# An early one-element gelu, two sums of halves behind a later product, and second-layer fills in four column tiles

## The chip, the cores and the metric

The kernel runs on one core of a Trainium2 chip. The core's engines work side by side, each from its own queue: PE (TensorE: matmuls, with its weight loads shown as PEld), DVE (VectorE), ACT (ScalarE), POOL (GpSimd) and SP (which here only issues DMAs). The metric is the device time of one execution in microseconds (us), the median of several runs. Before the change it is 344.38 us, the median of three runs (344.12 to 345.33).

## The reference

The kernel computes causal attention with a forgetting factor, and a two-layer perceptron with a tanh-gelu on its output.

```
q, k, v: (8, 8, 576, 64)   f: (8, 8, 576)   w_in: (512, 2048)   w_out: (2048, 512)
scores = q k^T / sqrt(64) + cum[query] - cum[key],  cum = cumsum(log(clip(f)))   (causal)
attn   = exp(scores - max) / (sum + 1e-09)
x      = (attn v), heads beside each other            -> (4608, 512)
h      = x @ w_in
g      = 0.5 h (1 + tanh(sqrt(2/pi) (h + 0.044715 h^3)))
out    = g @ w_out                                     -> (4608, 512) float32
```

Inputs and output are float32; the kernel multiplies in bfloat16 and accumulates in float32.

## The kernel before

**Attention** goes by quads, four heads of one batch at a time: 16 quads in all. For a quad `i`, `scores(i, r)` (line 224) makes the transposed scores in three rounds r = 0, 1, 2 of 512 columns each. Its matmuls have 32 rows, one head to each of the four row strips of the array. ACT then takes the exponential of each round with two instructions (line 232), into the tile `pt`. Masks on the diagonal run on POOL (line 238) or DVE. `denominators(i)`, called D, and `attn_out(i, x)`, called V and run for x = 0 and 1, multiply `pt` with the decay column or with the weighted values (line 292). Their matmuls have 128 rows and 32 (or 1) columns, one head to each of the four column strips: 24 matmuls each. Both write the PSUM tile `po`, of which there is one. DVE empties it: two transposes and a reciprocal behind D (lines 311 to 315), a product behind V (line 323), which writes `xT`, the input of the perceptron.

**The first layer** goes by chunks of 512 tokens: nine chunks, c = 0 to 8. `mlp_in(c, prs)` (line 334) makes 256 of the 2048 hidden features per call, with eight matmuls of 128x128 by 512, and ACT applies the gelu (line 341) into `gT`. Its PSUM tiles `ps_h` share two buffers (pool `psS`) with the scores.

**The second layer** of chunks 1 to 8 is one level of Strassen's scheme in Winograd's form: seven products of halves instead of eight. DVE prepares sums of halves: `weight_sums` once for the weights, and `gelu_sums(half, which)` for each chunk, in two halves of the features, each with four instructions. They are numbered 1 (`g1`, line 376), 2 (`g2`, line 378), 3 (the difference that takes the place of `a21` in `gT` and is read as `d1`, line 380) and 4 (`g4`, line 382), and run in the order 1, 3, 2, 4. `seven_products(c)` is a generator. Each step of it, called a fill here, is one matmul of 128x128 by 256 (line 397). A product takes 16 fills and a chunk 112. The products come in a fixed order: 1 is `a11 w11`, 2 is `a12 w21`, 3 is `g2 u2`, 4 is `d1 w3`, 5 is `g1 u1`, 6 is `a22 u4` and 7 is `g4 w22`. Two PSUM tiles `pa` and `pb` take turns. When a product ends, DVE copies it (`keep`, line 413), adds a kept copy to it or writes it out (`result`, lines 418 and 420), and SP starts the store. So product 3, which goes on in `pa`, has to wait until the copy of product 1 (`keep("p1", pa)`) is made.

**The order** is written out by hand, and each engine follows it in its own queue. For the first chunks it stands in the table FRONT: `S` is scores, `D` and `V` as above, `I` and `J` the first layer, `G` gelu_sums, `U` weight_sums, `F.c.n` and `f.c.n` n fills of chunk c, `X` load_exp. After FRONT a loop runs over c = 2 to 8. It makes the fills left over of chunk c-1, the eight `mlp_in` calls with `prepare` and the loads in between, the sums, and then the attention of two quads (`pair`), with the fills of chunk c between its parts. In `pair(i, j, c)` the order is S(i,0) D(j) 22 fills, S(i,1) V(j,0) 18, S(i,2) V(j,1) 16, S(i+1,0) D(i) 18, S(i+1,1) V(i,0) 9 V(i,1) 7, S(i+1,2). Ten fills stand ahead of it and the last 12 follow it. For c = 6 there is no quad i+1, and the second part is D(i) 18 V(i,0) V(i,1) 18. Chunks 7 and 8 have no attention beside them.

**Tables of ACT.** Exponentials and gelus need different function tables, and a change of table is an instruction of its own (ACT_TABLE_LOAD), put ahead of the first instruction that needs it. `load_exp` (line 196) is an exponential of one element, put ahead of the first real one, so that the table comes early. There is nothing of the kind for gelu.

**Column tiles.** A fill can be made in a second form. When the list `by_columns` is not empty, each fill becomes four matmuls of 128 rows and 32 columns, each with its own weight load, on the four column strips of the array. `out_part(c, n, tiled)` sets the list, and the table's word `f` calls it with tiled = 1. Before the change only some fills of chunk 0 (512 wide, line 459) are made so.

Of the kernel before, what the change touches and what calls it, by code (L numbers as in the profile page):

```python
# [10 lines left out]
AF = mybir.ActivationFunctionType  # L11
# [5 lines left out]
def kernel(  # L17
# [10 lines left out]
    nc = tc.nc  # L28

    B, H, S, D = q.shape  # L30
# [47 lines left out]
        LX.1.0@WO.2 TK.2 J.0.2 J.1.2 X LK.4 F.0.6 TK.3 B.3.256 S.2.0 LK.5 F.0.9 S.2.2 F.0.10 S.2.1 TQ.3 TQ.4 F.0.10 LV.2.0@LK.5 m.2.1 vw.2  # L78
        TK.4 S.3.0 f.0.1 M.2.2 CL.2 LQ.5 M.2.0 D.2 f.0.6 S.3.1 m.3.0 F.0.6 V.2.0 S.3.2 TK.5 LK.6 M.3.2 f.0.7 V.2.1 CL.3
        S.4.1 m.3.1 LQ.6 F.0.6 TQ.5 H.4.2.1 D.3 H.4.0.1 LQ.7 VW.4 H.4.0.0 V.3.1 v.3.0 f.0.3 H.4.2.0 CL.4 I.1.0 m.4.1 U.0 LV.2.1@LQ.5 I.1.4  # L80
        TQ.6 m.4.2.3 I.1.1 I.1.5 U.1 LV.3.0@LQ.7 m.4.2.2 TK.6 G.0 M.4.0 I.1.2 I.1.3 U.3 I.1.6 I.1.7 G.1 U.2 X F.1.14 S.5.0 F.1.28 S.5.1 D.4 M.5.0 F.1.16
        S.5.2 V.4.0 m.5.2.3 F.1.10 VW.5 V.4.1 CL.5 m.5.2.2 LQ.8 S.6.0 F.1.10 M.5.1 D.5 F.1.7 S.6.1 V.5.1 F.1.12 V.5.0 vw.6 S.6.2
        m.6.1 M.6.2.2 m.6.0 m.6.2.3 LK.7 LK.8 CL.6 LX.3.1@LK.6
    """

# [8 lines left out]
    def many(n, shape, dtype, name):  # L94
        return [singles.tile(shape, dtype, name=f"{name}{i}") for i in range(n)]
# [11 lines left out]
    vw = many(2, [128, NT + 1, 4, D], BF16, "vw")  # L107
# [13 lines left out]
    shift = singles.tile([128, 1], FP32, name="shift")  # L121
    idle = singles.tile([128, 512], BF16, name="idle")
    spare = singles.tile([1, 1], FP32, name="spare")
# [70 lines left out]
    def load_exp():  # L194

        nc.scalar.activation(spare, shift[0:1, :], AF.Exp)

    idle_ps = []

# [168 lines left out]
    def gelu_sums(half, which=(1, 3, 2, 4)):  # L368

        n = HF // 2  # L370
        f0, f1 = slice(n * half, n * half + n), slice(HF + n * half, HF + n * half + n)
        a11, a12 = gT[:, f0, 0:HC], gT[:, f1, 0:HC]
        a21, a22 = gT[:, f0, HC:CH], gT[:, f1, HC:CH]
        for k in which:
            if k == 1:
                nc.vector.tensor_add(g1[:, f0], a21, a22)  # L376
            if k == 2:
                nc.vector.tensor_sub(g2[:, f0], g1[:, f0], a11)
            if k == 3:
                nc.vector.tensor_sub(a21, a11, a21)  # L380
            if k == 4:
                nc.vector.tensor_sub(g4[:, f0], a12, g2[:, f0])

    def seven_products(c):

        r0, last = CH * c, c == NCH - 1
        a11, a12 = gT[:, 0:HF, 0:HC], gT[:, HF:, 0:HC]
        d1, a22 = gT[:, 0:HF, HC:], gT[:, HF:, HC:]
        w11, w3 = w_out_sb[:, 0:HF, 0:HD], w_out_sb[:, 0:HF, HD:]
        w21, w22 = w_out_sb[:, HF:, 0:HD], w_out_sb[:, HF:, HD:]  # L390

        def multiply(ps, x, w, first, then, ns=range(2), cols=(0, HD)):
            for n in ns:
                for j in range(HF):
                    width = 32 if by_columns else 128
                    for c0 in range(0, 128, width):
                        nc.tensor.matmul(ps[c0:c0 + width, n, cols[0]:cols[1]],  # L397
                                         x[:, j, 128 * n + c0:128 * n + c0 + width],
                                         w[:, j, cols[0]:cols[1]],
                                         start=(first and n == ns[0] and j == 0), stop=(j == HF - 1),  # L400
                                         skip_group_check=True)
                    if n == ns[-1] and j == HF - 1:
                        then()
                    yield

        def bank():
            return psM.tile([128, 2, HD], FP32, name="ps_w", tag="m")

        kept = {}

        def keep(name, ps):
            kept[name] = snap_pool.tile([128, 2, HD], FP32, name="snap", tag="snap")
            nc.vector.tensor_copy(kept[name], ps)  # L413

        def result(i, j, x, y=None):
            st = ostage_pool.tile([128, 2, HD], FP32, name="o_st", tag="o")
            if y is None:
                nc.vector.tensor_copy(st, x)
            else:
                nc.vector.tensor_add(st, x, y)  # L420
            nc.sync.dma_start(
                out=out[r0 + HC * i:r0 + HC * (i + 1), HD * j:HD * (j + 1)].rearrange("(n p) d -> p n d", p=128),
                in_=st)

        def corner():
            keep("v4", pa)
            result(1, 1, kept["p7"], kept["v4"])

        def piece(ps, n, cols):
            st = ostage_pool.tile([128, 2, HD], FP32, name="o_st", tag="o")  # L430
            s = slice(*cols)
            nc.vector.tensor_add(st[:, n, s], ps[:, n, s], kept["v4"][:, n, s])  # L432
            eng = nc.scalar if cols[0] else nc.sync
            eng.dma_start(out=out[r0 + 128 * n:r0 + 128 * n + 128, HD + cols[0]:HD + cols[1]], in_=st[:, n, s])

        pa, pb = bank(), bank()
        yield from multiply(pa, a11, w11, True, lambda: keep("p1", pa))
        yield from multiply(pb, a12, w21, True, lambda: result(0, 0, pb, kept["p1"]))
        yield from multiply(pa, g2, u2, False, lambda: keep("v2", pa))
        yield from multiply(pb, d1, w3, True, lambda: keep("p7", pb))  # L440
        yield from multiply(pa, g1, u1, False, corner)
        yield from multiply(pb, a22, u4, False, lambda: result(1, 0, pb, kept["v2"]))
        if not last:
            yield from multiply(pa, g4, w22, False, lambda: result(0, 1, pa))
            return
        for n, cols in ((0, (0, HD)), (1, (0, HD // 2)), (1, (HD // 2, HD))):
            ps = bank()
            yield from multiply(ps, g4, w22, True, lambda: piece(ps, n, cols), (n,), cols)

    def mlp_out(c):  # L450

        for n in range(CH // 128):
            r0 = CH * c + 128 * n
            st = ostage_pool.tile([128, D_MODEL], FP32, name="o_st", tag="o")
            pso = psM.tile([128, D_MODEL], FP32, name="pso", tag="m")
            for ft in range(N_FT):
                cols = 32 if by_columns else 128
                for c0 in range(0, 128, cols):
                    nc.tensor.matmul(pso[c0:c0 + cols, :],
                                     gT[:, ft, 128 * n + c0:128 * n + c0 + cols],  # L460
                                     w_out_sb[:, ft, :],
                                     start=(ft == 0), stop=(ft == N_FT - 1), skip_group_check=True)
                if ft == N_FT - 1:
                    nc.vector.tensor_copy(st, pso)
                    nc.sync.dma_start(out=out[r0:r0 + 128, :], in_=st)
                yield
# [61 lines left out]
    def pull(it, n):  # L528
        for _ in range(n):
            if next(it, False) is False:  # L530
                return
# [4 lines left out]
    def out_part(c, n, tiled=0):  # L536
        by_columns[:] = [True] * tiled
        pull(fills.setdefault(c, seven_products(c) if c else mlp_out(c)), n)
# [5 lines left out]
    def load_values(b, half):  # L544
# [31 lines left out]
        "I": lambda c, pr: mlp_in(c, (pr,)),  # L576
        "J": mlp_in_half,
        "U": weight_sums,
        "G": gelu_sums,
        "F": out_part,  # L580
        "f": lambda c, n: out_part(c, n, 1),
        "B": keep_busy,
        "X": load_exp,
    }

    def run(table):
# [10 lines left out]
    def beside(i, r, c, todo):  # L597

        if i is not None:
            scores(i, r)  # L600
        for n, x in enumerate(todo):
            if isinstance(x, int):
                out_part(c, x)
            else:
                x()
            if n == 0 and i is not None:
                after_scores(i, r)

    def after_scores(i, r):
        mask(i, r)  # L610
        if r == 1:
            make_vw(i, nc.gpsimd)
        if r == 2:
            copy_low(i)
# [25 lines left out]
    with tc.manual_schedule():  # L640
        setup()
        run(FRONT)
        for c in range(2, NCH):
            out_part(c - 1, CH)
            for pr in (0, 1):
                mlp_in(c, (pr,))
            if c + 1 < B:
                prepare(2 * c + 3, 2 * c + 4)
            if c + 2 < B:
                load_v(c + 2)  # L650
            for pr in (4, 5):
                mlp_in(c, (pr,))
            gelu_sums(0)
            for pr in (2, 3, 6, 7):
                mlp_in(c, (pr,))
            gelu_sums(1)
            if c + 1 < B:
                load_exp()
                out_part(c, 10)
                pair(2 * c + 3, 2 * c + 2, c)  # L660
        out_part(NCH - 1, CH)
# [30 lines left out]
```

## Time and profile before

The profiled execution took 344.71 us, of which its span, from the first to the last instruction, is 343.0 us. It lies 0.33 us over the median of the runs, so a difference worked out against the profiled execution is taken off the median as it is.

| engine | busy us | share of the span | instructions |
|---|---|---|---|
| PE | 322.6 | 94% | 3748 |
| PEld | 196.5 | 57% | 3768 |
| DVE | 199.3 | 58% | 307 |
| ACT | 191.2 | 56% | 201 |
| POOL | 110.6 | 32% | 155 |

The granted clock of PE is 0.996 of full speed on the mean. In the profile's lines the first number is the start and the second the time that the group took, both in us, then come engine, line, operation, output and inputs, tile (rows*columns for PE), shape and count. In square brackets stands how long the engine sat idle ahead of the group and what ended that. Matmuls are pipelined and their ends are modelled: the row of a matmul of 512 columns lasts 0.379 us, while the next one starts 0.2156 us behind it. So the pace is read from starts. A gap in the pipeline is a little longer than the idle time shown.

### The profile page before, as it was taken

What the parts mean: (1) busy time and instruction counts of PE and PEld (TensorE: products, weight loads), DVE (VectorE), ACT (ScalarE), POOL (GpSimd) and SP (SyncE); (2) the same over time, 40 slices, a digit from 0 to 9 for tenths busy, and PEclk for the clock granted to TensorE, in tenths of its full rate; (3) what the DMA queues carried; (4) which work ended last, traced back from release to release, by engine and by line L of the source; (5) the groups of instructions that cost most, each with busy time, mean ns of one, the idle gap of its engine ahead of it and who ended that gap; (6) DMA issues with size and microseconds to landing.
All of it is one profiled execution on the core that took longest, in us unless ns stands there. A gap on an engine that the chain in (4) does not pass through costs nothing. (4 is left out here: it accounts for less than half of the span.)

```text
span 343.0 us, 8601 instructions
## 1 busy us (share of the span) xinstructions
PE 322.6 (94%) x3748; PEld 196.5 (57%) x3768; DVE 199.3 (58%) x307; ACT 191.2 (56%) x201; POOL 110.6 (32%) x155
## 2 busy tenths in 40 slices
PE   3999999999899999999999999999999999989984
PEld 1458844445564466546654676456745774575574
DVE  4785059876686686737664566556634760452363
ACT  4784676777446566657466664675566605503500
POOL 8997470600506234601651145106410410000000
PEclk9999999999999999999999999999999999999998
DMA  7999999560316960490039211910110111002002
GB/s 131 218 221 179 204 226 212 98 154 2 65 44 127 226 145 31 117 216 10 32 112 201 58 33 65 212 26 32 51 45 0 34 36 59 1 32 92 0 32 92
DMA packets 44310, 33.21 MB, mean 97 GB/s; under 512 B 27488, under 2 KB 37856, under 8 KB 44272
## 3 DMA queue, kind: packets, MB, share of 16 engines
q0 software_dynamic: 8848, 16.58, 26.9%
q1 hardware_dynamic: 35280, 16.01, 17.4%
q8 instruction: 29, 0.48, 0.6%
q14 instruction: 9, 0.07, 0.1%
q10 hardware_dynamic: 144, 0.07, 0.1%
HBM read 36.85 MB, written 9.44 MB: 135 GB/s over the span
## 5 line engine op out<-in xcount | busy, mean ns | idle before, releaser
L232 ACT ACTIVATE pt<-ps_s 128x1024 bf16<-128x1024 f32 (+2 forms) x100 | 93.7, 988 | 52.9 <-PE ps_s L224 40.8
L334 PE MATMUL ps_h<-xT,w_in_sb 128*128 128x512 bf16 x496 | 111.8, 379 | 5.1 <-ACT gT L341 4.3
L341 ACT ACTIVATE gT<-ps_h 128x1024 bf16<-128x1024 f32 x64 | 64.9, 1024 | 51.4 <-PE ps_h L334 45.5
L334 PEld LDWEIGHTS <-w_in_sb 128*128 128x128 bf16 x512 | 49.9, 98 | 64.3 <-issue 6.4
L238 POOL TENSOR_SCALAR_AFFINE_SELECT pt<-pt 128x512 bf16<-128x512 bf16 (+3 forms) x65 | 38.4, 601 | 143.2 <-ACT pt L232 142.3
L397 PEld LDWEIGHTS <-gT 128*128 128x128 bf16 x512 | 48.3, 98 | 9.5 <-issue 0.2
L376 DVE TENSOR_TENSOR gsum<-gT 128x1024 bf16<-128x1024 bf16 x16 | 11.1, 692 | 66.3 <-ACT gT L341 66.3
L397 PE MATMUL ps_w<-w_out_sb,gT 128*128 128x256 bf16 x384 | 46.6, 273 | 0.0
L397 PEld LDWEIGHTS <-gsum 128*128 128x128 bf16 x392 | 36.3, 98 | 10.8 <-issue 5.4
L224 PE MATMUL ps_s<-qT,kT 32*128 32x64 bf16 (+5 forms) x896 | 36.9, 264 | 0.3 <-ACT pt L232 0.2
L397 PE MATMUL ps_w<-usum,gsum 128*128 128x256 bf16 x256 | 32.0, 273 | 3.5 <-DVE snap L413 3.5
L182 POOL TENSOR_TENSOR vw<-v_nat,wT 128x1280 bf16<-128x1280 f32 (+1 forms) x13 | 30.0, 2310 | 0.1
L165 DVE STREAM_TRANSPOSE kT<-k_c 128x576 f32<-128x576 f32 x16 | 19.9, 1247 | 16.0 <-DMA k_c<-in_k_dram 15.8
L413 DVE COPY snap<-ps_w 128x512 f32<-128x512 f32 x32 | 21.6, 676 | 12.9 <-PE ps_w L397 12.9
L224 PEld LDWEIGHTS <-kT 32*128 32x128 bf16 x896 | 17.0, 93 | 17.3 <-issue 11.5
L323 DVE TENSOR_TENSOR xT<-po,rb 128x576 bf16<-128x576 f32 x26 | 19.6, 754 | 11.9 <-PE po L292 11.8
L292 PE MATMUL po<-pt,vw 128*32 128x64 bf16 (+4 forms) x624 | 22.5, 279 | 0.3 <-DVE xT L323 0.3
L165 DVE STREAM_TRANSPOSE qT<-q_c 128x576 f32<-128x576 f32 x16 | 19.9, 1244 | 1.8 <-DMA q_c<-in_q_dram 1.1
L292 PEld LDWEIGHTS <-vw 128*32 128x32 bf16 x672 | 13.6, 96 | 12.2 <-issue 5.5
L341 ACT ACT_TABLE_LOAD x7 | 9.0, 1283 | 16.3 <-issue 16.3
L397 PE MATMUL ps_w<-usum,gT 128*128 128x256 bf16 x128 | 17.0, 273 | 0.0
L136 POOL DMA_DIRECT2D v_nat<-in_v_dram x20 | 15.3, 778 | 5.0 <-DMA w_out_sb<-in_moe_w_out_dram 5.0
(79 smaller groups left out, 276.1 us busy)
## 6 DMA issues: line engine op xcount, KB each, us to landing
out_dram<-o_st SPq DMA_DIRECT2D x35, 256.0 KB, 2.3
k_c<-in_k_dram POOLq DMA_DIRECT2D x16, 288.0 KB, 6.2
q_c<-in_q_dram POOLq DMA_DIRECT2D x16, 288.0 KB, 7.4
v_nat<-in_v_dram SPq DMA_DIRECT2D x16, 256.0 KB, 8.5
w_in_sb<-in_moe_w_in_dram POOLq DMA_DIRECT2D x4, 512.0 KB, 8.5
w_out_sb<-in_moe_w_out_dram POOLq DMA_DIRECT2D x4, 512.0 KB, 8.9
v_nat<-in_v_dram SPq DMA_DIRECT2D x16, 128.0 KB, 3.5
v_nat<-in_v_dram POOLq DMA_DIRECT2D x13, 128.0 KB, 7.4
```

The costliest lines, as they stand in the source:

```text
L136: ins.append(eng.dma_start(out=v_nat[b % 2][:n, t, h0:h0 + nh, :], in_=v[b, h0:h0 + nh, 128 * t:128 * t + n, :].rearrange("h p d -> p h d"),))
L165: nc.vector.transpose(out=dst.rearrange("p s c -> p (s c)").bitcast(FP32) .rearrange("p (t a) -> p a t", a=S // 32), in_=src.rearrange("p ...
L182: eng.tensor_mul(vw[i % 2][:, t0:t1], vb[:, t0:t1, h0:h0 + 4, :], wT[:, i, t0:t1, :].unsqueeze(3).to_broadcast([128, t1 - t0, 4, D]))
L224: nc.tensor.matmul(tiles[h // 2][:, h % 2, c0:c0 + nq], key_columns(i, key, h, c), qq[32 * h:32 * h + 32, q0:q0 + nq, c], start=(c == 0 an ...
L232: nc.scalar.activation(p[:, 2 * g:2 * g + 2, off:off + n], t[:, :, 0:n], AF.Exp, scale=scale)
L238: nc.gpsimd.affine_select(out=x, in_=x, compare_op=ALU.is_ge, fill=0.0, base=0, pattern=pattern, channel_multiplier=-1)
L292: nc.tensor.matmul(po[r0:r0 + w.shape[-1], 448 + q0:448 + q0 + nq], w, p[:, h, col:col + nq], start=(key in (0, "low")), stop=(key in ("lo ...
L323: nc.vector.tensor_mul(xT[:, 2 * u + x, S * b + s0:S * b + s1], po, rbs[i, part])
L334: nc.tensor.matmul(ph[:, j, :], w_in_sb[:, dt, 128 * ft:128 * ft + 128], xT[:, dt, CH * c:CH * (c + 1)], start=(dt == 0), stop=(dt == N_DT ...
L341: nc.scalar.activation(gT[:, 2 * pr:2 * pr + 2, :], ph, AF.Gelu_apprx_tanh)
L397: nc.tensor.matmul(ps[c0:c0 + width, n, cols[0]:cols[1]], x[:, j, 128 * n + c0:128 * n + c0 + width], w[:, j, cols[0]:cols[1]], start=(fir ...
L413: nc.vector.tensor_copy(kept[name], ps)
```

## The change

- A new function `load_gelu` runs a gelu of one element. It is called at the top of the loop for c = 2 to 7, which is behind the last exponentials of the pair of chunk c-1, and ahead of the left-over fills and of the first `mlp_in`.
- For the second half of the features `gelu_sums` makes only sums 1 and 2 at its old place, in the loop (c = 2 to 8) and in FRONT (`G.1` becomes `G.1.1.2`). Sums 3 and 4 of that half run in the new `first_corner`, at the end of product 2, behind `result(0, 0, ...)`.
- The fills inside `pair` (`beside`) and six groups of chunk 1's fills in FRONT use the form with four column tiles. The ten fills ahead of `pair`, the left-over fills at the top of the loop and the fills of chunks 7 and 8 stay as they were. Every fill inside `pair` so issues eight PE instructions (four weight loads, four matmuls) in place of two.

```
@@ FRONT
-        ... G.0 M.4.0 I.1.2 I.1.3 U.3 I.1.6 I.1.7 G.1 U.2 X F.1.14 S.5.0 F.1.28 S.5.1 D.4 M.5.0 F.1.16
-        S.5.2 V.4.0 m.5.2.3 F.1.10 VW.5 V.4.1 CL.5 m.5.2.2 LQ.8 S.6.0 F.1.10 M.5.1 D.5 F.1.7 S.6.1 V.5.1 F.1.12 V.5.0 vw.6 S.6.2
+        ... G.0 M.4.0 I.1.2 I.1.3 U.3 I.1.6 I.1.7 G.1.1.2 U.2 X F.1.14 S.5.0 f.1.28 S.5.1 D.4 M.5.0 f.1.16
+        S.5.2 V.4.0 m.5.2.3 f.1.10 VW.5 V.4.1 CL.5 m.5.2.2 LQ.8 S.6.0 f.1.10 M.5.1 D.5 f.1.7 S.6.1 V.5.1 f.1.12 V.5.0 vw.6 S.6.2
@@
+    def load_gelu():
+
+        nc.scalar.activation(spare, shift[0:1, :], AF.Gelu_apprx_tanh)
@@ seven_products
+        def first_corner():
+            result(0, 0, pb, kept["p1"])
+            gelu_sums(1, (3, 4))
+
...
-        yield from multiply(pb, a12, w21, True, lambda: result(0, 0, pb, kept["p1"]))
+        yield from multiply(pb, a12, w21, True, first_corner)
@@ ops
-        "G": gelu_sums,
+        "G": lambda half, *which: gelu_sums(half, which or (1, 3, 2, 4)),
...
+        "Y": load_gelu,
@@ beside
-                out_part(c, x)
+                out_part(c, x, 1)
@@ the loop
         for c in range(2, NCH):
+            if c <= B - 1:
+                load_gelu()
             out_part(c - 1, CH)
...
-            gelu_sums(1)
+            gelu_sums(1, (1, 2))
```

## The prediction

> **What bounds the kernel now.** I read the page's first part, then the waits, then the order of time around each wait. PE is busy for 94% of the span, so the matmuls' own stream sets the end, and a change counts by what it takes out of that stream or puts in.
>
> ```profile
> span 343.0 us, 8601 instructions
> PE 322.6 (94%) x3748; PEld 196.5 (57%) x3768; DVE 199.3 (58%) x307; ACT 191.2 (56%) x201; POOL 110.6 (32%) x155
> ```
>
> The list of waits names two things on which PE stands again and again behind chunk 0; the last number is the longest single wait.
>
> ```profile
> PE ps_h L334 <- ACT gT L341: 4.3, 6, 0.7
> ...
> PE ps_w L397 <- DVE snap L413: 3.5, 3, 1.4
> ```
>
> The first, in order of time at the start of chunk 3: the last exponentials, the table load, the first gelus, and PE's first layer, which stops after 16 matmuls because both `ps_h` buffers are full.
>
> ```profile
> 139.12 1.94 ACT L232 ACTIVATE pt<-ps_s 128x1024 bf16<-128x1024 f32 x2 [2.17 <-issue]
> ...
> 140.29 3.62 PE L334 MATMUL ps_h<-xT,w_in_sb 128*128 128x512 bf16 x15
> ...
> 142.25 1.28 ACT L341 ACT_TABLE_LOAD   x1 [1.19 <-issue]
> ...
> 143.55 1.94 ACT L341 ACTIVATE gT<-ps_h 128x1024 bf16<-128x1024 f32 x2
> ...
> 144.62 10.52 PE L334 MATMUL ps_h<-xT,w_in_sb 128*128 128x512 bf16 x47 [0.71 <-ACT gT L341]
> ```
>
> ACT is idle for 1.19 us and loads the table only when the first `ps_h` is ready. The second wait, at the end of the last chunk: four sums, then the copy of product 1, then product 3.
>
> ```profile
> 324.78 3.66 PE L397 MATMUL ps_w<-w_out_sb,gT 128*128 128x256 bf16 x32
> ...
> 326.82 0.69 DVE L380 TENSOR_TENSOR gT<-gT 128x1024 bf16<-128x1024 bf16 x1
> 327.43 0.68 DVE L378 TENSOR_TENSOR gsum<-gsum,gT 128x1024 bf16<-128x1024 bf16 x1
> 328.15 0.69 DVE L382 TENSOR_TENSOR gsum<-gT,gsum 128x1024 bf16<-128x1024 bf16 x1
> 328.76 0.68 DVE L413 COPY snap<-ps_w 128x512 f32<-128x512 f32 x1
> 329.49 1.91 PE L397 MATMUL ps_w<-usum,gsum 128*128 128x256 bf16 x16 [1.06 <-DVE snap L413]
> ```
>
> Third, PE's own order inside attention. Chunk 0 already has a tiled group (28 matmuls, 7 fills of 512) ahead of V; chunk 3 has V between scores and an untiled group.
>
> ```profile
> 57.59 1.69 PE L459 MATMUL pso<-w_out_sb,gT 128*32 128x512 bf16 x28
> 59.11 0.85 PE L292 MATMUL po<-pt,vw 128*32 128x512 bf16 x24
> ...
> 65.08 0.87 PE L292 MATMUL ps_o<-pt,vw 128*32 128x512 bf16 x24
> 65.76 0.83 PE L459 MATMUL pso<-w_out_sb,gT 128*32 128x512 bf16 x12
> ...
> 160.80 0.86 PE L292 MATMUL po<-pt,vw 128*32 128x512 bf16 x24
> 161.60 1.92 PE L397 MATMUL ps_w<-usum,gsum 128*128 128x256 bf16 x16
> ```
>
> V followed by a tiled group takes 65.76 - 65.08 = 0.68 us from start to start; V followed by an untiled one 161.60 - 160.80 = 0.80. So a change of tile shape costs PE 0.12 us. Untiled fills pay it too: at 171.74 nine fills ahead of a V last until 172.83, 1.09 us, where 9 x 0.109 = 0.98. (0.109 is the untiled fill's pace: 32 fills in the tail, product to product 1.744 us for 16.)
>
> **Part 1, the early gelu.** It adds to ACT six one-element gelus (`load_exp`'s twin takes 0.20 us) and only moves six table loads (1.28 us each). In chunk 3 the exponentials end at 141.06. Load and small gelu need 1.41 us together (120.18 to the next exponential at 121.58 in the `load_exp` row), so ACT is free at 142.47, 0.22 after `ps_h` is ready. The first gelu ends at 143.49 in place of 144.55. PE wants that buffer after 16 matmuls of 0.2156 us: 140.29 + 3.45 = 143.74, and gets it with 0.2 to spare. Its stream today resumes at 144.62: a gap of 0.88 (the 0.71 shown leaves out the pipeline). All six places look the same, at chunk 7 with far more room (ACT idle for 10.14 us): 6 x 0.88 = **5.3 us off**. Cover: ACT's idle time between last exponential and first `ps_h`. If that shrank by over 0.2 us, the wait would come back bit by bit. Behind it ACT is paced by PE (1.73 us per pair of features against 1.02 per gelu).
>
> **Part 2, the moved sums.** Nothing is added; two DVE instructions of 0.69 us move per chunk. In the last chunk sums 1 and 2 would end about 327.5 and the copy about 328.2. Product 3 can follow product 2 at 324.78 + 32 x 0.109 = 328.27, against 329.49: 1.2 us off, and the same in chunk 7 (302.23 against 301.02). In FRONT the weight sum U.2 (1.22) stands between, so the copy would end near 85.45 in place of 86.71: 1.3 us off, 0.25 of the wait left. Together **3.7 us off**. Next in line: sum 3 has to be made ahead of product 4. In the tail `result(0,0)` ends about 329.15, sum 3 at 329.86, and product 4 starts at 328.27 + 1.74 = 330.01: 0.15 us to spare. Sum 4 holds back the copy of product 3 to about 331.2; product 5, which needs it, starts at 331.76. In chunks 2 to 6 PE doesn't wait on the sums; there the pair stands on DVE between `result(0,0)` and the xT product of V(j,0), which it makes 0.5 us later (127.25 in place of 126.78 in chunk 2). V(j,1), which needs that PSUM tile, starts near 127.9: hidden by 0.6 us, and that is what it costs beyond. No DMA moves: SP's store follows `result` as before, POOL's queue is untouched.
>
> **Part 3, tiled fills.** First, what a tiled fill costs. A 256-wide one isn't in the trace. The tiled 512-wide one keeps the untiled pace: 59.11 - 57.59 = 1.52 for 7, 0.217 each. V itself is 24 tiled matmuls of 512, 64, 448, 320, 192 and 64 columns: 1600 columns a strip in 0.68 us, 0.667 of streaming and 0.002 a step, so weight loads hide even behind steps far under 256. From these rows a tiled fill is 0.109 us, like the untiled.
>
> Saved, 0.12 us at each V- or D-to-fill and fill-to-V border. A pair has seven: 0.84. One is cut short: V(i,1) can't start before xT of V(i,0) leaves PSUM (136.53 in chunk 2; V(i,1) starts at 136.74, so 0.16 of 0.24 is had): 0.76 for each of chunks 2 to 5, 3.0. Chunk 6 has six borders, one new one to its untiled rest, and D(15), which already waits for POOL's mask: 0.5. FRONT has seven, of which the three between D.5 and V.5.0 fall to DVE's chain, on which V.5.0 waits today (0.32 at 101.18): 0.5. **4.0 us off**.
>
> What it adds: 83 fills in FRONT, 4 x 90 in chunks 2 to 5, 92 in chunk 6, 535 in all, six more PE instructions each: 3210 on top of 7516. That is the unknown. In one pair (24 + 16 + 16 + 24 + 16 + 16 score matmuls, 144 of D and V, 360 of fills, and as many loads: 1232 instructions) PE's sequencer must deliver one each 14.7 ns for 18.1 us. What the trace shows over stretches:
>
> ```profile
> 51.33:53.31 1.98, 1.98 (x65) 1.08 (x68) 1.98 (x4) 1.18 (x2) 0.00 (x0) 1.00 1.07 238
> ...
> 62.65:65.98 3.33, 3.33 (x100) 2.08 (x96) 2.51 (x5) 2.91 (x3) 2.87 (x2) 1.00 0.88 136
> 93.71:99.25 5.54, 5.54 (x130) 3.42 (x129) 4.25 (x9) 2.65 (x4) 0.00 (x0) 1.00 0.01 3
> ```
>
> (Stretch, its length, then busy time and count for PE and PEld.) 133 instructions in 1.98 us is 14.9 ns, 196 in 3.33 is 17.0, 259 in 5.54 is 21.4. These are rates that the work asked for, and every gap in them is a change of tile shape or a semaphore wait. So the cost lies between -4.0 us (the sequencer keeps up) and, if 21.4 ns were its limit, 1232 x 21.4 ns = 26.4 in place of today's 18.9 us a pair: +7.5, times 535/90 = 5.9 pairs, +44 us. I take -4.0: inside V, eight instructions start within 28 ns at each 64-wide step, and the shortest stretch runs at the rate wanted with no stall of the sequencer.
>
> A rule speaks against this. The Trainium skill (Runtime: NRT & Kernel Launch, Instruction fetch mechanics) gives the sequencers an issue floor of about 20 cycles per instruction. At the 1.2 GHz that TensorE: Matmul & The Clock Gate (Wait - 56ns, not 53.3ns?) states for it that is, as an estimate, 16.7 ns; a pair would take 20.6 us, and part 3 would cost some 10 us and eat the other two. The 14.9 ns row is under that floor, but short enough that the PE queue of 64 (same page, queue depths) could have been filled beforehand.
>
> **Sum:** -5.3 - 3.7 - 4.0 = -13.0 on 344.71 of the profiled execution, the same on the median of 344.38: 331.4, said as **331.5 us**.
>
> **Rivals.** *(a) The borders' gain goes to other waits.* `po` is a single buffer, masks on POOL end just ahead of D; two places show it already. Part 3 gives 0: 344.4 - 9.0 = 335.4. Against it: in the pairs the xT products end 0.6 us or more ahead of the next use, but for the one counted. *(b) The sequencer is the bound.* Place: the pairs. Price: (1232 x t - 18.9 us) x 5.9. At t = 16.6 ns it eats the 9.0 us of parts 1 and 2; above that the kernel is slower than before. At the 17.0 of the middle stretch it is +12.1: **347.5 us**. For it: nothing in the trace holds such a rate over 2 us. Against: the rows above. Between 14.7 and 16.6 ns lies 331 to 344; I put 339 for that. *(c) The early gelu doesn't do what it says:* the load still falls between the first `ps_h` and its gelu, or ACT's margin of 0.2 us goes. Then 331.4 + 5.3 = 336.7. Against: `load_exp` does the same thing seven times, its load straight behind the last gelu.
>
> **How the numbers follow.** Forecast 0.70 (own range 329.8 to 334.5: the margins of 0.15 and 0.2 us lost, or a half of part 3), (a) 0.12, (b) 0.10, the rates in between 0.04, (c) 0.04. From 329.5 to 341 lie the forecast, (a), (c) and most of the rates in between; (b) and the tails outside, under 2 in 10. 0.5% is 1.7 us, about what can be told from no change: faster 0.88, same 0.03, slower 0.09.
>
> **What would show it.** PE's wait on line 341 gone, and six table loads within 0.05 us of the last exponential; the copy of product 1 two DVE instructions behind the last gelu in chunks 7 and 8, and product 3 without a wait of 1.06; V-to-fill 0.68 in place of 0.80, 18 tiled fills still 1.96 and not 2.4. Wrong if tiled fills take over 0.109 us each, with PE gaps that no semaphore ends.

## The result, and the profile after

The changed kernel takes 333.22 us (median of four runs, 332.61 to 333.51), against 344.45 for the kernel before beside it (344.12 to 345.33). The ratio is 0.9668, with a 95% interval of 0.9645 to 0.969. That is 11.2 us off, where the forecast had 13.0: the direction is right, the time lies inside the range, and 1.8 us of the gain are missing.

All line numbers from 198 on are shifted in the changed kernel, by four up to the middle of the second layer and a little more behind it: `scores` is 228, D and V 296, the first layer 338, its gelu 345, the four sums 380 to 386, a fill 401, a copy 417. The page's first part and its queue of instructions, of the kernel after:

```profile
span 331.5 us, 11765 instructions
...
PE 317.6 (96%) x5353; PEld 202.1 (61%) x5373; DVE 201.0 (61%) x307; ACT 192.5 (58%) x207; POOL 110.3 (33%) x155
...
q8 instruction: 42, 0.69, 0.9%
```

PE is still the bound, more so than before. It has 1605 more matmuls and 1605 more weight loads, the 3210 instructions that were counted ahead, and its idle time fell from 343.0 - 322.6 = 20.4 us to 13.9. The last line is the queue that brings instructions from memory: it had 29 packets and 0.48 MB before. The list of PE's waits behind chunk 0 no longer has the gelu in it, and the copies stand in it for 0.2 us in place of 3.5. A wait for D's transposes (`den`) is new (total, times, longest one, in us):

```profile
PE po L296 <- DVE den L315: 0.3, 1, 0.3
...
PE ps_w L401 <- DVE snap L417: 0.2, 1, 0.2
```

**Part 1** in order of time, at the start of chunk 3, of the kernel after:

```profile
137.30 1.94 ACT L236 ACTIVATE pt<-ps_s 128x1024 bf16<-128x1024 f32 x2 [1.97 <-issue]
...
138.47 11.82 PE L338 MATMUL ps_h<-xT,w_in_sb 128*128 128x512 bf16 x52
...
139.26 1.28 ACT L200 ACT_TABLE_LOAD   x1
...
140.55 0.20 ACT L200 ACTIVATE spare<-shift 1x1 f32<-1x1 f32 x1
140.66 1.00 ACT L345 ACTIVATE gT<-ps_h 128x1024 bf16<-128x1024 f32 x1
```

The table load follows the last exponential (137.30 + 1.94 = 139.24) by 0.02 us, as do the five others (0.01 to 0.02). The first layer, which broke off after 16 matmuls before (15 in the row, as a few records are missing), runs on: from its start to the ten fills behind it are 13.81 us, 64 matmuls of 0.2156.

**Part 2**, the last chunk, of the kernel after:

```profile
314.61 3.66 PE L401 MATMUL ps_w<-w_out_sb,gT 128*128 128x256 bf16 x32
...
316.65 0.69 DVE L382 TENSOR_TENSOR gsum<-gsum,gT 128x1024 bf16<-128x1024 bf16 x1
317.26 0.68 DVE L417 COPY snap<-ps_w 128x512 f32<-128x512 f32 x1
...
318.10 1.91 PE L401 MATMUL ps_w<-usum,gsum 128*128 128x256 bf16 x16
...
318.91 0.68 DVE L384 TENSOR_TENSOR gT<-gT 128x1024 bf16<-128x1024 bf16 x1
...
319.85 1.91 PE L401 MATMUL ps_w<-w_out_sb,gT 128*128 128x256 bf16 x16
```

Product 3 starts 318.10 - 314.61 = 3.49 us behind product 1, which is 32 fills of 0.109 with nothing between. Sum 3 ends at 319.59, 0.26 ahead of product 4 that reads it (0.15 was predicted).

**Part 3**, the pair of chunk 3, of the kernel after: V, then tiled fills; and the one border that was counted as cut short.

```profile
157.94 0.87 PE L296 MATMUL po<-pt,vw 128*32 128x512 bf16 x24
...
158.63 1.92 PE L401 MATMUL ps_w<-usum,gsum 128*32 128x256 bf16 x64
...
160.38 0.39 PE L401 MATMUL ps_w<-w_out_sb,gT 128*32 128x256 bf16 x8
...
168.68 0.76 DVE L327 TENSOR_TENSOR xT<-po,rb 128x576 bf16<-128x576 f32 x1
...
169.50 0.87 PE L296 MATMUL po<-pt,vw 128*32 128x512 bf16 x24
```

V to fill takes 0.69 from start to start (0.80 before). 64 instructions of the tiled form are 16 fills, and the next group starts 160.38 - 158.63 = 1.75 behind: 0.109 each, the untiled pace. V(i,1) starts 0.06 behind the end of the xT product (169.44), so this border is cut short, as foreseen.

Where the time went, from starts of PE's groups in the two traces. "FRONT" is the stretch from `F.1.14` to the first layer of chunk 2, a first layer reaches to the ten fills behind it, a pair from there to the next first layer. Chunks 7 and 8 are their fills, the last one up to the start of its last matmul:

| stretch | before, us | after, us | difference | forecast |
|---|---|---|---|---|
| FRONT | 23.22 | 22.48 | -0.74 | -1.8 |
| first layers, chunks 2 to 7, each | 14.69 (14.47 in 7) | 13.81 (13.60) | 6 x -0.88 = -5.28 | -5.3 |
| pair of chunk 2 | 21.41 | 20.98 | -0.43 | -0.76 |
| pairs of chunks 3, 4, 5, together | 64.24 | 62.00 | -2.24 | -2.28 |
| chunk 6's quad | 19.78 | 19.26 | -0.52 | -0.5 |
| fills of chunk 7 | 13.44 | 12.23 | -1.21 | -1.2 |
| fills of chunk 8 | 13.64 | 12.42 | -1.22 | -1.2 |

The differences add up to -11.64. Five of the rows are within 0.05 us of the forecast. What is missing sits in the other two: 1.06 us in FRONT and 0.33 in the pair of chunk 2.

### The profile page after: what moved, and what is told of

Its sections match the earlier page's. It is cut to its first block, busy times and chain, and to the rows that moved or that the text cites. A ratio compares the mean times of both kernels' runs of the same rounds, so it can differ in the third digit from the quotient of the medians.

```text
span 331.5 us, 11765 instructions
## 1 busy us (share of the span) xinstructions
PE 317.6 (96%) x5353; PEld 202.1 (61%) x5373; DVE 201.0 (61%) x307; ACT 192.5 (58%) x207; POOL 110.3 (33%) x155
## 4 chain that ended last, share of the span: by engine, by line
PE 87%; DVE 4%; DMA 3%; POOL 2%; issue 1%; ACT 1%; POOLq 0%; DVEq 0%; ACTq 0%
PE ps_h L338 33%; PE ps_w L401 27%; PE po L296 8%; PE ps_s L228 8%; PE ps_h L355 4%; PE pso L467 4%; DMA v_nat<-in_v_dram 3%; PE po_m L282 1%; ACT pt L236 1%; DVE gsum L386 1%; POOL vw L182 1%; DMA out_dram<-o_st 1%; POOL v_nat L136 0%; DVE xT L327 0%; DVE den L315 0%
## 5 line engine op out<-in xcount | busy, mean ns | idle before, releaser
L401 PEld LDWEIGHTS <-gT 128*32 128x32 bf16 (+1 forms) x1472 | 51.5, 97 | 4.5 <-issue 0.2
L401 PE MATMUL ps_w<-w_out_sb,gT 128*32 128x256 bf16 (+1 forms) x1056 | 46.7, 273 | 0.0
L401 PEld LDWEIGHTS <-gsum 128*32 128x32 bf16 (+1 forms) x1037 | 38.4, 97 | 4.3 <-issue 2.1
L401 PE MATMUL ps_w<-usum,gsum 128*32 128x256 bf16 (+1 forms) x832 | 32.1, 273 | 0.2 <-DVE snap L417 0.2
L296 PEld LDWEIGHTS <-vw 128*32 128x32 bf16 x672 | 14.5, 96 | 11.8 <-issue 5.0
L401 PE MATMUL ps_w<-usum,gT 128*32 128x256 bf16 (+1 forms) x416 | 17.1, 273 | 0.0
L401 PE MATMUL ps_w<-w_out_sb,gsum 128*128 128x256 bf16 (+2 forms) x205 | 16.6, 269 | 0.0
```

Source lines behind the costliest of these rows:

```text
L296: nc.tensor.matmul(po[r0:r0 + w.shape[-1], 448 + q0:448 + q0 + nq], w, p[:, h, col:col + nq], start=(key in (0, "low")), stop=(key in ("lo ...
L401: nc.tensor.matmul(ps[c0:c0 + width, n, cols[0]:cols[1]], x[:, j, 128 * n + c0:128 * n + c0 + width], w[:, j, cols[0]:cols[1]], start=(fir ...
```

## The experiments

Three questions were open: whether each part does what the sum says it does (and not another part), where the gain of FRONT and of chunk 2 went, and, the unknown of the prediction, how near PE's supply of instructions is to being the bound.

### One part at a time

Three kernels, each the kernel before with one part of the change.

**Only the early gelu.**

```
@@ the kernel before
+    def load_gelu():
+
+        nc.scalar.activation(spare, shift[0:1, :], AF.Gelu_apprx_tanh)
...
         for c in range(2, NCH):
+            if c <= B - 1:
+                load_gelu()
             out_part(c - 1, CH)
```

> The kernel before with the early one-element gelu alone (no moved sums, no tiled fills). The prediction's step: PE's six gaps of 0.88 us at line 341 go and nothing takes their place: 344.45 - 5.3 = 339.1 us. Rival: the gain is a loan that attention gives back, because exponentials or masks end later than PE then wants them: 340 to 342 us, with new idle time of PE ahead of scores or D.

Measured: 339.31 us (338.98 to 342.71), against 344.88 for the kernel before, ratio 0.9852 [0.98, 0.9903], so 5.6 us off where 5.3 were worked out. Every first layer takes 13.81 in place of 14.69, and the pairs behind them take 21.36 and 21.35, against 21.41: nothing is given back, and rival (c) falls. The 0.05 us lie in a pair's first score round, which now takes 0.71 us from start to start in place of 0.76. The waits of this kernel still hold the second item of the old list, whole:

```profile
PE ps_w L401 <- DVE snap L417: 3.5, 3, 1.4
```

**Only the moved sums.**

```
@@ the kernel before, FRONT
-        ... U.3 I.1.6 I.1.7 G.1 U.2 X F.1.14 ...
+        ... U.3 I.1.6 I.1.7 G.1.1.2 U.2 X F.1.14 ...
@@ seven_products
+        def first_corner():
+            result(0, 0, pb, kept["p1"])
+            gelu_sums(1, (3, 4))
...
-        yield from multiply(pb, a12, w21, True, lambda: result(0, 0, pb, kept["p1"]))
+        yield from multiply(pb, a12, w21, True, first_corner)
@@ ops
-        "G": gelu_sums,
+        "G": lambda half, *which: gelu_sums(half, which or (1, 3, 2, 4)),
@@ the loop
-            gelu_sums(1)
+            gelu_sums(1, (1, 2))
```

> The kernel before with the two late sums of the second half moved behind product 2, alone. The prediction's step: 3.7 us off (1.2 in each of chunks 7 and 8, 1.3 in FRONT): 340.75 us. What the trace of the change suggests instead: in FRONT sums 3 and 4 now run beside POOL's vw product and take 1.16 and 2.82 us in place of 0.69, so that D's transposes are late and about 0.9 of the 1.3 is lost: 2.4 + 0.4 = 2.8 us off, 341.6 us.

Measured: 341.69 us (341.51 to 342.33), ratio 0.9902 [0.9878, 0.9926], 3.2 off. Chunks 7 and 8 have their whole gain (12.23 and 12.42). FRONT has only 0.63 of its 1.3. Sums 3 and 4 took 1.16 and 2.81 us there in place of 0.69 each, and the first transpose behind D, which stands behind them in DVE's queue, started only at 89.79. Product 3 gets what was forecast: from the 18 fills ahead of it (83.10) to its start (85.32) are 2.22 us, where it was 3.54, and 18 fills need 1.96. So 1.32 us are won there and about 0.25 of the wait are left. But D's chain on DVE is late now: V.4.0 starts 0.33 us late, and the ten fills behind it, which need a copy that stands behind that chain, take 1.56 in place of 1.20.

**Only the tiled fills.**

```
@@ the kernel before, FRONT
-        F.1.28 ... F.1.16 ... F.1.10 ... F.1.10 ... F.1.7 ... F.1.12
+        f.1.28 ... f.1.16 ... f.1.10 ... f.1.10 ... f.1.7 ... f.1.12
@@ beside
-                out_part(c, x)
+                out_part(c, x, 1)
```

> The kernel before with the tiled fills alone. The prediction's step: 0.12 us at each border, 4.0 us off in all: 340.45 us, each pair of chunks 3 to 5 shorter by 0.76 (from the start of the ten fills to the first matmul of the next first layer 20.65 us in place of 21.41). Rival: the 3210 added instructions cost something that joint running hid: 341.5 to 344 us, with gaps of PE that no semaphore ends.

Measured: 342.00 us (341.38 to 344.79), ratio 0.9903 [0.9875, 0.9931]: 2.9 off, less than the 4.0 forecast. (The profiled execution is the one of 344.79; what it lost lies in chunk 0, ahead of all stretches compared here.) FRONT gives 0.41 of 0.5, but a pair 0.59 in place of 0.76. Over half of the difference stands at product 3 of chunk 3:

```profile
162.80 0.86 PE L292 MATMUL po<-pt,vw 128*32 128x512 bf16 x24
162.88 0.65 DVE L413 COPY snap<-ps_w 128x512 f32<-128x512 f32 x1
...
163.58 1.93 PE L397 MATMUL ps_w<-usum,gsum 128*32 128x256 bf16 x64
```

The copy of product 1 ends at 163.53, because all four sums are ahead of it on DVE, and product 3 starts right behind: 0.78 from V to fill in place of the 0.69 of the kernel after. In the kernel after, with the sums moved, the copy ends at 157.57, ahead of V itself, and a pair gives 0.75. Of these, 0.05 are the first score round, which came with the early gelu, so the borders give 0.70 on top of part 2, and less without it. The three kernels alone make 5.57 + 3.19 + 2.88 = 11.64, and the whole change 11.2 to 11.5, so the parts help each other in the pairs and take from each other in FRONT (0.63 + 0.41 alone, 0.74 together).

### Where FRONT's gain went

In the kernel after, product 3 starts 2.22 us behind the 18 fills ahead of it, as with the sums alone. So the 1.3 us of the forecast are there, and something behind them takes them back. First the kernel before, then FRONT of the kernel after, in order of time:

```profile
83.22 2.14 PE L397 MATMUL ps_w<-w_out_sb,gT 128*128 128x256 bf16 x18
...
85.58 1.50 POOL L238 TENSOR_SCALAR_AFFINE_SELECT pt<-pt 64x256 bf16<-64x256 bf16 x2 [18.43 <-ACT pt L232]
...
86.76 1.25 PE L397 MATMUL ps_w<-usum,gsum 128*128 128x256 bf16 x10 [1.40 <-DVE snap L413]
...
87.17 2.33 POOL L182 TENSOR_TENSOR vw<-v_nat,wT 128x1280 bf16<-128x1280 f32 x1
```

```profile
83.45 2.15 PE L401 MATMUL ps_w<-w_out_sb,gT 128*32 128x256 bf16 x72
...
85.67 1.27 PE L401 MATMUL ps_w<-usum,gsum 128*32 128x256 bf16 x40
...
85.81 1.12 POOL L242 TENSOR_SCALAR_AFFINE_SELECT pt<-pt 64x256 bf16<-64x256 bf16 x2 [18.42 <-ACT pt L236]
86.31 1.16 DVE L384 TENSOR_TENSOR gT<-gT 128x1024 bf16<-128x1024 bf16 x1
...
87.02 2.64 POOL L182 TENSOR_TENSOR vw<-v_nat,wT 128x1280 bf16<-128x1280 f32 x1
87.39 2.82 DVE L386 TENSOR_TENSOR gsum<-gT,gsum 128x1024 bf16<-128x1024 bf16 x1
...
90.13 0.77 DVE L315 STREAM_TRANSPOSE den<-po 128x576 f32<-128x576 f32 x1
...
90.96 0.87 PE L296 MATMUL po<-pt,vw 128*32 128x512 bf16 x24 [0.34 <-DVE den L315]
...
92.65 0.62 PE L401 MATMUL ps_w<-usum,gsum 128*32 128x256 bf16 x16 [0.17 <-DVE snap L417]
```

Sum 4 lies beside POOL's product `VW.5` (`vw`, line 182) and takes four times as long as alone; sum 3 lies beside two masks on POOL. The transpose that empties `po` then starts at 90.13, and V.4.0 waits for it: the score round ahead of it takes 0.98 us from start to start in place of 0.56. The ten fills behind V.4.0 lose 0.48 more (1.68 us in place of 1.20), because those at 92.65 wait for a copy that stands behind the same chain. Together that is 0.90 of the 1.06 us. If POOL's product is the cause, sum 4 must come back to 0.69 when that product runs at another time. The next kernel moves it, with nothing else:

```
@@ the kernel after, FRONT
-        ... G.0 M.4.0 I.1.2 ... S.5.2 V.4.0 m.5.2.3 f.1.10 VW.5 V.4.1 ...
+        ... G.0 M.4.0 VW.5 I.1.2 ... S.5.2 V.4.0 m.5.2.3 f.1.10 V.4.1 ...
```

> The changed kernel with one line of FRONT's order altered: POOL's product VW.5 is issued behind the mask M.4.0, some 10 us earlier, so that POOL is idle while DVE makes sums 3 and 4 of chunk 1. If POOL's product is what slows these two sums, they take 0.69 us each, V.4.0's wait of 0.34 and the wait on the copy in front of the fills go, and the time is 333.2 - 0.9 = 332.3 us. If the sums are slow for another reason (their place behind the PSUM reads, say), they stay at 1.2 and 2.8 us and the time is 333.2 us.

Measured: 331.94 us (331.66 to 332.44), ratio 0.9618 [0.9594, 0.9641]. FRONT takes 21.48, which is 1.74 less than before: the forecast's 1.8. The rows of this kernel:

```profile
72.76 2.33 POOL L182 TENSOR_TENSOR vw<-v_nat,wT 128x1280 bf16<-128x1280 f32 x1 [6.17 <-DMA v_nat<-in_v_dram]
...
74.75 0.89 DVE L380 TENSOR_TENSOR gsum<-gT 128x1024 bf16<-128x1024 bf16 x1 [2.07 <-ACT gT L345]
...
85.02 1.14 POOL L242 TENSOR_SCALAR_AFFINE_SELECT pt<-pt 64x256 bf16<-64x256 bf16 x2 [9.92 <-ACT pt L236]
85.51 1.18 DVE L384 TENSOR_TENSOR gT<-gT 128x1024 bf16<-128x1024 bf16 x1
...
86.61 0.68 DVE L386 TENSOR_TENSOR gsum<-gT,gsum 128x1024 bf16<-128x1024 bf16 x1
...
89.74 0.87 PE L296 MATMUL po<-pt,vw 128*32 128x512 bf16 x24
```

Sum 4 takes 0.68 again, V.4.0 waits for nothing, and the ten fills behind it take 1.10. The masks still stretch sum 3, and the moved product now stretches sum 1 of the first half, by 0.2, where nothing waits for it. In all four places the sum ends the same time behind POOL's instruction: sum 4 at 90.21 and POOL at 89.66 (0.55), sum 3 at 87.47 and 86.93 (0.54), and in the last kernel sum 1 at 75.64 and 75.09 (0.55), sum 3 at 86.69 and 86.16 (0.53). That end at a constant distance, whatever the sum's start, fits a sum that stands until POOL is done and then runs, and not one that runs slowly. It goes the other way too: the product that begins beside sum 3 takes 2.64 us in place of 2.33. An instruction with only one operand in SBUF is not held. In the kernel before, a `result`, with its other operand in PSUM, starts in the middle of such a product and takes its usual time, as the product does:

```profile
137.69 2.33 POOL L182 TENSOR_TENSOR vw<-v_nat,wT 128x1280 bf16<-128x1280 f32 x1
...
138.33 0.68 DVE L420 TENSOR_TENSOR o_st<-ps_w,snap 128x512 f32<-128x512 f32 x1
```

The Trainium skill (SBUF — State Buffer, SBUF: two separate sides) says just this of the port pair that the two engines share: a DVE instruction with two SBUF inputs and a GpSimd one that reads SBUF lock each other out for a whole instruction; whichever starts first has the pair. These rows agree with it.

### The gap in chunk 2

The pair of chunk 2 has one stall that the other pairs lack. PE and its weight loads in the third score round of the kernel after (in chunk 3 the same round takes 0.64):

```profile
125.91 0.95 PE L228 MATMUL ps_s<-qT,kT 32*128 32x320 bf16 x16
...
126.49 0.10 PEld L228 LDWEIGHTS <-kT 32*128 32x128 bf16 x4 [0.31 <-issue]
```

No semaphore ends it ("issue"). The kernel with the early product has the stall at the same PE instruction (0.63), and so had the changed kernel when it ran a second time, unaltered:

> The changed kernel itself, unaltered, beside the others on one chip: 333.2 us, and the gap in chunk 2's score round at the same instruction, of another length (0.3 to 0.6 us), if it depends on when the instruction fetch falls among the loads.

Measured: 333.50 us (332.82 to 336.63), ratio 0.9669 [0.963, 0.9707], with a stall of 0.60 at that instruction and 21.26 us for the pair. So it belongs to the kernel, and its length varies. In the trace's records of the instruction queue, a 16-KB block for PE starts at 119.02 and the next one only at 124.06, where later ones in the pair follow each other by 3.6 to 3.7 us (124.06, 127.64, 131.36, 134.98). PE goes on at 126.49, 2.4 us behind the start of that block (2.7 and 2.6 in the two other traces). Up to 124 the DMA engines are full. Here are two stretches of the kernel after (last but one column: the share of the 16 DMA engines):

```profile
119.00:122.00 3.00, 3.00 (x116) 2.50 (x112) 2.76 (x5) 2.99 (x4) 0.00 (x0) 1.00 1.11 208
122.00:124.00 2.00, 2.00 (x72) 1.24 (x68) 1.91 (x4) 0.73 (x2) 1.07 (x2) 1.00 1.02 214
```

About half of what fills them from 119 to 124 is SP's queue, with the load of V's next batch, which the loop issues in chunk 2; the other half is POOL's queue (q, k and more of v). The next kernel issues V's load earlier, in FRONT:

```
@@ the kernel with the early product, FRONT
-        ... G.1.1.2 U.2 X F.1.14 ...
+        ... G.1.1.2 U.2 LV.4.0 LV.4.1 X F.1.14 ...
@@ the loop
-            if c + 2 < B:
+            if 2 < c < B - 2:
```

> The kernel of e4 (VW.5 early), with the loads of v for batch 4 issued in FRONT, behind U.2, in place of the loop's c = 2. In the traces of the change and of e4, PE stands once without any semaphore, in the middle of a score round of chunk 2's first quad (0.33 and 0.63 us, at the same instruction), while the 16 DMA engines are full of loads and an instruction fetch lies among them. Theory: PE has run out of fetched instructions. With 1.2 MB of loads moved to a stretch where the DMA engines are idle, the gap goes: 0.3 to 0.6 us under e4, 331.4 us. Rival: the gap is something in the score round itself (its keys, its PSUM buffer) and stays at 0.3 us or more: 331.9 us.

Measured: 331.67 us (331.11 to 331.77), ratio 0.9599 [0.9559, 0.964]. The DMA engines are idle from 119 to 122, the block starts at 122.41, 3.4 us behind the one before it, and the round and the pair (20.66) are like the others:

```profile
125.15 0.64 PE L228 MATMUL ps_s<-qT,kT 32*128 32x320 bf16 x16
```

```profile
119.00:122.00 3.00, 3.00 (x120) 2.60 (x108) 2.79 (x5) 2.26 (x4) 0.59 (x2) 1.00 0.01 1
```

That the stall goes when the transfers go is shown. That the block came late because of them is the likely link, but it was not taken apart further. One more trace fits it. The kernel with the tiled fills alone has the same loads and no stall: chunk 2's pair takes 20.83 there, chunk 3's 20.82. Its PE comes to the place later, as the wait on the gelu still stands ahead of it, and its block starts at 127.08, 3.6 us behind the one before, just when the share of the DMA engines falls (1.09 from 126 to 127, 0.38 from 127 to 128). The medians of this kernel and of the one with the early product lie 0.27 us apart with ranges that overlap, so the gain of this step is only read from the stretch (0.6 us): the start of FRONT varies by about 1 us between runs.

### How near the supply of instructions is

Tiled fills beside nothing show what PE's supply allows. Chunk 7's fills were tiled, eight instructions each, and chunk 8's were cut into two halves of 128 columns besides, sixteen each.

```
@@ the kernel after, multiply
-                    for c0 in range(0, 128, width):
+                    step = (cols[1] - cols[0]) // max(1, len(by_columns))
+                    for a in range(cols[0], cols[1], step):
+                        for c0 in range(0, 128, width):
...
@@ the loop and the end
-            out_part(c - 1, CH)
+            out_part(c - 1, CH, 1 if c == NCH - 1 else 0)
...
-        out_part(NCH - 1, CH)
+        out_part(NCH - 1, CH, 2)
```

> The changed kernel with the fills of chunks 7 and 8 tiled as well, where no attention lies between and 112 fills follow each other. In chunk 7 each fill is eight PE instructions (13.6 ns each at the pace of 0.109 us a fill); in chunk 8 each of the four column tiles is made as two matmuls of 128 moving columns, sixteen instructions a fill (6.8 ns each; its last product keeps its own split). If PE's instruction supply holds 13.6 ns, chunk 7's fills take 12.23 us as now, plus two changes of tile shape: 12.5 us. The prediction's rival (b) at 17.0 ns would make that 15.2 us, at 16.7 ns 15.0 us. In chunk 8 a limit above 6.8 ns shows: product to product 1.744 us if there is none, 2.56 us at 10 ns, 3.5 us at 13.6 ns.

Measured: 345.42 us, one run. Chunk 7, then the beginning of chunk 8:

```profile
292.46 1.92 PE L403 MATMUL ps_w<-usum,gsum 128*32 128x256 bf16 x64
294.21 1.92 PE L403 MATMUL ps_w<-w_out_sb,gT 128*32 128x256 bf16 x64
...
315.22 3.76 PE L403 MATMUL ps_w<-w_out_sb,gT 128*32 128x128 bf16 x256
318.80 0.33 PE L403 MATMUL ps_w<-usum,gsum 128*32 128x128 bf16 x9
320.11 1.86 PE L403 MATMUL ps_w<-usum,gsum 128*32 128x128 bf16 x119 [0.98 <-issue]
```

Chunk 7 runs 128 instructions in 1.75 us, 13.7 ns each, for all its 896 with no stall, and takes 12.34 us. Chunk 8 runs its first 512 in 3.58 us, 7.0 ns each, with as little trouble. Then it stands, six times, 8.9 us in all. The stalls end exactly 256 PE instructions (matmuls and loads) apart, at 320.11, 324.11, 327.57, 331.30, 335.57 and 339.03: 3.78 us for each 256 on the mean, or 14.8 ns an instruction. A block of the instruction queue starts 2.2 to 2.6 us ahead of the end of each stall, and the next one 1.1 to 2.0 us after PE goes on. So the sequencer has no floor near 15 ns. What limits a long stream is the fetching of blocks: PE runs through some 530 instructions, the block that starts at 314.00 among them, and then gets one block at a time. The Trainium skill (Runtime: NRT & Kernel Launch, Instruction fetch mechanics) has the fetch hidden behind an issue floor of about 20 cycles. Here PE's instructions go out in under half of the 16.7 ns that the prediction estimated from it, and the fetch shows.

The same in the pairs of chunks 3 to 6, where the fills share PE with attention:

```
@@ the kernel after, with the halves of the diff above, beside
-                out_part(c, x, 1)
+                out_part(c, x, 2 if c > 2 else 1)
```

> The changed kernel with the tiled fills of chunks 3 to 6 beside attention made of sixteen PE instructions in place of eight (each column tile as two matmuls of 128 moving columns). From the first of the ten fills to the next first layer a pair then has about 1996 PE instructions, 7.8 blocks of 256. In e6, once the blocks fetched ahead were used up, PE got one block each 3.75 us on the mean (stalls ended at 320.11, 324.11, 327.57, 331.30, 335.57 and 339.03). If that supply bounds PE beside attention too, a pair takes between 5.8 x 3.75 + 2 x 1.75 = 25.3 us (two blocks ready) and 29.3 us (none), in place of 20.66, with gaps 256 instructions apart that no semaphore ends: 350 to 368 us in all. If e6's stalls belonged to the tail alone, the pair takes 20.66 + 90 x 0.003 = 20.9 us, 334.5 us in all.

Measured: 368.62 us, one run, beside 344.78 of the kernel before. The pairs of chunks 3, 4 and 5 take 30.41, 29.33 and 28.59 us, against 20.66; the first stalls of chunk 3 (18 such waits in the fills of the whole kernel, 19.8 us):

```profile
155.33 2.29 PE L403 MATMUL ps_w<-w_out_sb,gT 128*32 128x128 bf16 x149
158.77 0.57 PE L403 MATMUL ps_w<-w_out_sb,gT 128*32 128x128 bf16 x27 [1.15 <-issue]
```

Again 256 instructions lie between two stalls, 3.73 us as a rule (158.77, 162.50, 166.23, 169.96, 173.69). Chunk 3's pair lies 1.1 us above the 29.3 that were expected at most; why is open. So a loss of rival (b)'s kind is real, though it is blocks that come late and not a slow sequencer: the kernel is 24 us slower than before when a fill has sixteen instructions.

### A kernel that follows from it

The two losses mended, and the fills dealt so that DVE's chain ends ahead of PE: more of them ahead of the steps that wait for it. A group of chunk 0's fills is tiled as well.

```
@@ the kernel with V's batch early, FRONT
-        ... D.2 f.0.6 S.3.1 m.3.0 F.0.6 V.2.0 ... S.6.0 f.1.10 M.5.1 D.5 f.1.7 S.6.1 ...
+        ... D.2 f.0.6 S.3.1 m.3.0 f.0.6 V.2.0 ... S.6.0 f.1.12 M.5.1 D.5 f.1.5 S.6.1 ...
@@ pair
-        beside(i, 2, c, [V(j, 1), 16])
+        beside(i, 2, c, [V(j, 1), 16 if i + 1 < NQ else 20])
...
-            beside(i + 1, 1, c, [V(i, 0), 9, V(i, 1), 7])
+            beside(i + 1, 1, c, [V(i, 0), 10, V(i, 1), 6])
...
-            beside(None, 0, c, [D(i), 18, V(i, 0), V(i, 1, True), 18])
+            beside(None, 0, c, [D(i), 14, V(i, 0), V(i, 1, True), 18])
```

> The kernel of e5 with four small moves of fills, each against a wait that the trace of the change still shows: ten and six fills around V(i,1) in place of nine and seven (0.07 us in each of chunks 2 to 5), 20 and 14 in place of 16 and 18 around D(15) (0.4 us on POOL's mask), 12 and 5 in place of 10 and 7 around D.5 in FRONT (0.5 us on DVE's chain ahead of V.5.0), and F.0.6 ahead of V.2.0 tiled (0.12). If each wait goes without a new one: 1.3 us under e5, 330.1 us. If DVE's chain only moves its place: 330.7 us or more.

Measured: 330.59 us (329.85 to 330.99), ratio 0.9571 [0.9542, 0.9599], the fastest kernel here. By stretches: pairs 20.59 to 20.60 in place of 20.65 and chunk 6 18.83 in place of 19.26, both as expected, and FRONT 21.26 in place of 21.48, less than half of the 0.5 expected. There V.5.0's wait for DVE (0.54) is gone, and V.5.1 waits 0.42 for D's chain, which it did not in the kernel before it.

## Why the prediction was right and wrong

**What bounds the kernel** was read rightly: PE's stream, with two kinds of waits in it and the borders between tile shapes. The first kind went whole and the second but for some 0.25 us in FRONT, and PE's idle time fell by 6.5 us.

**Part 1** (5.3 us) holds in every number: 0.87 or 0.88 in each of six first layers, the load 0.02 us behind the last exponential, small gelu and load 1.40 us together, nothing given back in the pairs. The ACT row of `load_exp`, which already did the same thing, was the right row to price it by.

**Part 2** (3.7 us) holds in chunks 7 and 8; the spare ahead of product 4 was 0.26 us where 0.15 was said. Its term for FRONT, "1.3 us off, 0.25 of the wait left", is right for product 3 itself: the copy of product 1 came as early as worked out, 1.32 us are won and 0.25 are left. What failed is that nothing behind it was to take the gain back. The step priced both moved sums at 0.69 in their new place and looked at DVE's queue and PE's readers alone. Beside them, in POOL's rows of the kernel before, stood the masks at 85.58 and the product `VW.5` at 87.17 for 2.33 us. A sign of it was there: those two masks took 1.50 us beside the weight sum U.2 (84.89 to 86.11), and 1.14 in the pairs. POOL's instructions hold DVE's sums from SBUF, so sums 3 and 4 took 1.16 and 2.82 us, D's chain behind them was late, and V.4.0 and the fills behind it lost 0.90. Alone, the sums gave 0.63 there; with the product elsewhere FRONT gave 1.74, the sum of both forecast terms (1.3 + 0.5) to 0.1. The prediction looked at what is queued behind a moved step on DVE and wrote that "POOL's queue is untouched", which is true. It did not ask what POOL's instructions do to the moved step itself.

**Part 3** (4.0 us) is right in its row-made price: tiled fills keep 0.109 us, a border is worth 0.11 (0.12 was said), and the cut-short one is cut short. That three pairs give 0.75 each where 0.76 stood is in part luck: 0.05 of it belongs to the early gelu, and the borders give 0.70. They do so only with part 2 in place; alone a pair gives 0.59, so the terms were not as separate as the sum made them. Its term for chunk 2 failed by 0.33 (0.6 in the second run). Here PE stood once without a semaphore, 2.4 us behind the start of a late block of instructions, in a stretch where the DMA engines were full. The prediction had asked whether PE's sequencer is fast enough, which it is, and not when the instructions arrive.

**Rival (b)** was given 0.10 with a price from stretch rates, and the issue floor that the prediction set beside it, 16.7 ns, does not hold here (7.0 ns were measured). What there is in its place is the fetch, and its size is now measured: a stream that outruns its supply gets 14.8 ns an instruction, not 17.0 or 21.4. Put into the prediction's own formula, 1232 x 14.8 ns is 18.2 us, against the 18.1 needed. So the outcome that the prediction took stood, but nearer to the limit than its three rows told: what the trace of before could not show was that the limit exists at all, since none of its stretches reached it. **Rival (a)** holds in small where part 3 stands alone, at product 3, and in FRONT; not in the pairs of the changed kernel. **Rival (c)** holds nowhere.

Of the 1.8 us missed, 1.06 + 0.33 lie in the two places. The rest, 0.4, is less than the start of FRONT varies from run to run (80.40 to 81.43 us in the traces, but for the one that lost time in chunk 0). 0.23 of it are just that: FRONT starts at 80.97 in the profiled execution before and at 81.20 in the one after.

## What to carry to other kernels

When an instruction is moved on DVE, read POOL's rows at its new place as well as DVE's queue: here a sum of two SBUF operands ended 0.53 to 0.55 us behind whatever product or mask POOL was running. When a change multiplies the instructions of an engine, count them per 256 and compare with the pace at which its blocks are fetched (here some 3.75 us each), and look at what the DMA engines do at that time. A one-element activation behind the last use of the old table hid a table load of 1.28 us at the price of 0.2 us on an engine that had the time.

## What the runs showed of the hardware

- A bfloat16 sum of 128x1024 from SBUF takes 0.69 us on DVE alone, 2.82 beside POOL's product of 128x1280 and 1.16 to 1.18 beside two masks of 64x256. In each case it ends 0.53 to 0.55 us behind POOL's instruction.
- PE takes instructions at 7.0 ns each for 512 of them, and then one block of 256 per 3.78 us on the mean (14.8 ns each). At 13.7 ns it ran 896 without a stall. How much longer a stream at 13.7 ns, or one at a rate between these, runs before it stalls was not measured.
- A weight load of 32 columns and its matmul of 128 columns cost almost no time of their own at 7.0 ns an instruction: cutting a fill into sixteen instructions leaves its pace at 3.58 us for 32 fills (0.112 each, against 0.109) as long as blocks are in hand.
